# A gated-state attention block with a maxout FFN: start-up order, two subtractions moved to GpSimd, and the last outputs stored by quarters

## The chip, the cores and the metric

The kernel runs on one core of one Trainium2 chip. The metric is the device time of one launch in microseconds (us), the median of three runs.

## The reference

First a recurrence over 768 tokens for each of 4 batches and 8 heads (head size 48), then a feed-forward block of three products, an elementwise maximum and a fourth product over the 3072 tokens.

```python
f = 1.0 / (1.0 + np.exp(-f_logit))                 # B=4, H=8, S=768, D=48
for t in range(S):
    state = f[:, :, t, :, None] * state + np.einsum('bhd,bhe->bhde', k[:, :, t], v[:, :, t])
    y[:, :, t] = np.einsum('bhd,bhde->bhe', q[:, :, t], state)
x = np.ascontiguousarray(y.transpose(0, 2, 1, 3)).reshape(B * S, H * D)    # 3072 x 384
h = np.maximum(np.maximum(x @ w1, x @ w2), x @ w3)                         # 384 x 768 each
return h @ w_out                                                           # 768 x 384
```

## The kernel before

**Units and groups.** The attention part works in 24 *units* (u) of 64 tokens of two batches, all heads. A unit passes through `sigmoids` (the gates), `scan`, `after` (the scaled keys kh), `before` (the scaled queries qh), `keys` (keys turned for the state), `pairs` (key-query products, masked on VectorE), `values` (those times v), `sums` (the unit's addition to the state), `carry` (the old state times the unit's decay, on GpSimd), and `y_by_tokens` with `x_of_tokens` in the first four units, `finish` in the others. Four units make a group of 512 tokens, whose feed-forward block is put out piecemeal between the steps of later units: `fill(ns)` takes steps of a generator until their estimated cost has been used up. The first group has its own generator, `ffn_first`; the other five use `inputs_by_pairs` (the three input products by a scheme with fewer multiplications on sums and differences of weights and tokens) and `outputs_by_pairs` (the output product, likewise).

**Order.** The order of all instructions on every engine is the program's own, written out under a manual schedule; each engine executes its instructions in that order and waits on semaphores where a tile is not ready. DMAs are issued from SP's queue, a few from ACT's.

**Weights.** The weights arrive as 64-bit floating-point numbers and are turned to 32 bits in 24 pieces of 128 columns (n = 0 to 17 for w1, w2, w3 in turn, 18 to 23 for w_out). `round_begin(n)` is ACT's part: for n of 3 and over three instructions (L240, L241 on the upper words, L244 on the lower), for n under 3 only L244. `round_end(n)` is VectorE's part (L251 and L252 for n under 3, L254 for the others) and a sum on GpSimd (L258). `round_to(count)` runs, for every n up to count, round_begin of piece n+1 and round_end of piece n, and then the differences: w2 - w1 of a column block (n = 1, 4, 7 and so on) at once on GpSimd, w3 - w1 (n = 2, 5, 8 and so on) one piece later on VectorE, both by `apart` (L699). `ffn_first` uses them: its first product needs the difference of piece 1, its second that of piece 2, its third and fourth those of pieces 4 and 5, its fifth and sixth those of 7 and 8. The list `ROUNDED` tells how far the pieces are brought in each of its steps, and `TURNED` in which steps a block of w1 is transposed (`turn`, L720, copied by ACT in L721).

**Banks.** `ps_a` holds one tile, used by `pairs` and, in the first units, by `sums`; in units 0 and 1 the state is copied out of it by ACT (L442), in later ones added on VectorE (L444). `ps_tr` and `ps_f` have two tiles each, given out in turn. The 1x1 product at the head of `y_by_tokens` (L473) takes one of `ps_f`.

**The start.** The order around units 1 to 3 is written out by hand (L964 to L1004): y and x of unit 1, rounding of pieces 0 to 2, scan, pairs and carry of unit 3, and then the steps of `ffn_first`, one at each `fill(STEP)`.

**The end.** `outputs_by_pairs` multiplies blocks of 192 columns for two tiles of 128 tokens at a time into three banks: a of `ps_f`, b and c of `ps_tr`. `into(bank, p, ...)` puts tile pair p's block there, three matrix products each. Bank results are added to `partial` sums on VectorE (`add`, L619), on GpSimd (L655) or copied by ACT (L670) into `o_four`, four tiles of 128 x 384. `o_of(n, c)` is the column half c of the tiles n and n+2 in it. In the last group (`last`) the four tiles are written by `store` (two DMAs of 64 rows each) as soon as all columns of a tile are done: tiles 1 and 3 after L670, tile 0 and tile 2 after one half each of the last add; the second halves of tiles 2 and 3 go by ACT's queue, all others by SP's.

Of the kernel before, what the change touches and what calls it, by code (L numbers as in the profile page):

```python
# [46 lines left out]
C = 64  # L47
# [8 lines left out]
def kernel(  # L56
# [12 lines left out]
    nc = tc.nc  # L69
    B, H, S, D = q.shape  # L70
    HP = H // 2
    NU = B // 2 * (S // C)
    UT = 2 * C
    DM = H * D
    NK = DM // 128
    DFF = moe_w1.shape[1]
    NJ = DFF // 128
    GRP = 4
# [11 lines left out]
    def fast():  # L90
        ctx = ExitStack()
        with ctx:
# [64 lines left out]
            one = (nc.sync, nc.sync)  # L157
# [203 lines left out]
            def keys(u):  # L361

                if u < min(BY_ROWS, NU - 2):
                    kh = ready[u]["kh"]
                    tr_s = ps_tr.tile([UT, HP, 128], FP32, name="tr")
                    for hp in range(HP):
                        nc.tensor.transpose(tr_s[:, hp, :], kh[:, hp].rearrange("p a t -> p (a t)"), ident)
                    ks = work.tile([UT, H, DP], FP32, name="ks")
                    nc.scalar.copy(ks.rearrange("s h d -> s (h d)"), tr_s.rearrange("s a d -> s (a d)"))
                    ready[u]["ks"] = ks  # L370
# [51 lines left out]
            def sums(u):  # L422

                d, v_ld = ready[u], v_tiles[u % NLD]
                y = d["y"]
                if u < NU - 2:


                    apart = u < GRP
                    if apart:  # L430
                        y = ps_a.tile([128, 2, 512], FP32, name="a")
                    Y = HP * C
                    for hp in range(HP):
                        for par, a in FOUR:
                            s = slice(a * C, (a + 1) * C)
                            nc.tensor.matmul(y[par * DP:(par + 1) * DP, a, Y + hp * D:Y + (hp + 1) * D],  # L436
                                             lhsT=d["ks"][s, 2 * hp + par, :], rhs=v_ld[s, 2 * hp + par, 0:D],
                                             start=apart and hp == 0, stop=(hp == HP - 1), skip_group_check=True)
                    ds = y[:, :, Y:Y + HP * D]
                    new = states[u % 2].rearrange("p (a h) d -> p a (h d)", a=2)  # L440
                    if u < 2:
                        nc.scalar.copy(new, ds)  # L442
                    else:
                        nc.vector.tensor_tensor(new, ds, d["state"].rearrange("p (a h) d -> p a (h d)", a=2), op=ALU.add)  # L444
# [106 lines left out]
            def store(u, o):  # L551
                c, bp = divmod(u, 2)
                for a in range(2):
                    t0 = (2 * bp + a) * S + c * C
                    last = u >= NU - 2 and a
                    (nc.scalar if last else nc.sync).dma_start(out=out[t0:t0 + C, :], in_=o[a * C:(a + 1) * C, :])

            def outputs(hm, xT, i):
                p = bank()
# [16 lines left out]
            HJ, HD = NJ // 2, DM // 2  # L576
# [22 lines left out]
            def outputs_by_pairs(g, hm, xT):  # L599
                tile_of = lambda p, n: slice((2 * p + n) * UT, (2 * p + n + 1) * UT)  # L600
                A = lambda k, n: lambda p: hm[:, k::2, tile_of(p, n)]
                X = lambda n: lambda p: xT[:, 0:NK, tile_of(p, n)]
                s1, s2, s4 = (lambda p, t=t: t[:, :, p * UT:(p + 1) * UT] for t in s_mix)
                lin = [w_lin[:, :, n * HD:(n + 1) * HD] for n in range(2)]
                o_of = lambda n, c: o_four.rearrange("t (p n) c -> t n p c", p=2)[:, n, :, c * HD:(c + 1) * HD]
                last = g == NU // GRP - 1
                begun = set()

                def into(b, p, lhs, rhs):
                    for k in range(HJ):  # L610
                        nc.tensor.matmul(b[:, p * HD:(p + 1) * HD], lhsT=lhs(p)[:, k], rhs=rhs[:, k],  # L611
                                         start=id(b) not in begun, stop=(k == HJ - 1), skip_group_check=True)
                        begun.add(id(b))

                def read(b, n):
                    nc.scalar.copy(partial[n], b[:, 0:DM])  # L616

                def add(out, b, n, at=slice(0, 2)):
                    nc.vector.tensor_tensor(out[:, at], pairs_of(b[:, 0:DM])[:, at], pairs_of(partial[n])[:, at], op=ALU.add)  # L619

                COST = HJ * HD * COLUMN
                a, b, c = bank(), bank(True), bank(True)
                into(b, 0, X(0), lin[0])
                yield COST
                into(b, 1, X(0), lin[0])
                yield COST
                into(a, 0, A(0, 0), corner(0, 0))
                yield COST
                into(b, 0, A(1, 0), corner(1, 0))
                yield COST  # L630
                into(a, 1, A(0, 0), corner(0, 0))
                read(a, 0)
                yield COST
                into(b, 1, A(1, 0), corner(1, 0))
                add(o_of(0, 0), b, 0)
                yield COST
                into(a, 0, s2, w_mix[1])
                yield COST
                into(a, 1, s2, w_mix[1])
                read(a, 1)  # L640
                yield COST
                into(c, 0, s1, w_mix[0])
                yield COST
                into(c, 1, s1, w_mix[0])
                nc.scalar.copy(tops[:, 2], c[:, 0:DM])
                yield COST
                into(a, 0, A(0, 1), w_mix[2])
                yield COST
                into(a, 1, A(0, 1), w_mix[2])
                yield COST  # L650
                into(a, 0, X(1), lin[1])
                yield COST
                into(a, 1, X(1), lin[1])
                read(a, 2)
                nc.gpsimd.tensor_tensor(o_of(1, 1), pairs_of(tops[:, 2]), pairs_of(partial[2]), op=ALU.add)  # L655
                yield COST
                into(c, 0, X(0), lin[1])
                yield COST
                into(c, 1, X(0), lin[1])
                yield COST  # L660
                into(a, 0, A(1, 1), w_mix[3])
                yield COST
                into(a, 1, A(1, 1), w_mix[3])
                if g + 1 in packed:
                    sums_of_x(g + 1)
                yield COST
                into(a, 0, X(1), w_mix[4])
                yield COST
                into(a, 1, X(1), w_mix[4])
                nc.scalar.copy(o_of(1, 0), pairs_of(a[:, 0:DM]))  # L670
                if last:
                    for p in range(2):
                        store(g * GRP + 2 * p + 1, o_four[:, 2 * p + 1])
                yield COST
                into(c, 0, s4, corner(1, 1))
                if last:
                    add(o_of(0, 1), c, 1, slice(0, 1))
                    store(g * GRP, o_four[:, 0])
                yield COST
                into(c, 1, s4, corner(1, 1))  # L680
                if last:
                    add(o_of(0, 1), c, 1, slice(1, 2))
                    store(g * GRP + 2, o_four[:, 2])
                else:
                    add(o_of(0, 1), c, 1)
                    late.extend((g * GRP + i, o_four[:, i]) for i in (1, 3, 0, 2))
                yield COST

            late = []

# [4 lines left out]
            def apart(n, engine):  # L695
# [2 lines left out]
                piece = w_in[i][:, :, j * 128:(j + 1) * 128]  # L698
                engine.tensor_tensor(piece, piece, w_in[0][:, :, j * 128:(j + 1) * 128], op=ALU.subtract)  # L699

            rounded = [0]

            def round_to(count):

                for n in range(rounded[0], min(count, len(pieces))):
                    if n + 1 < len(pieces):
                        round_begin(n + 1)
                    round_end(n)
                    if n < 3 * NJ and n % 3 == 1:
                        apart(n, nc.gpsimd)  # L710
                    if n <= 3 * NJ and n and n % 3 == 0:
                        apart(n - 1, nc.vector)
                    rounded[0] = n + 1

# [212 lines left out]
            with tc.manual_schedule():  # L927
# [39 lines left out]
                values(1)  # L967
                y_by_tokens(1)
                keys(2)
                round_to(2)  # L970
                sums(1)
                x_of_tokens(1, xT)
                scan(3)
                pairs(2)
                after(3)
                carry(3)
                round_to(3)
                before(3)
                values(2)
# [2 lines left out]
                keys(3)  # L982
                sums(2)
                fill(STEP)
                y_by_tokens(2)
                pairs(3)
                fill(STEP)
# [342 lines left out]
```

## Time and profile before

| what | us |
|---|---|
| median of 3 runs (426.74 to 427.01) | 426.76 |
| the profiled execution, its own time | 427.35 |
| its span, first to last instruction | 425.5 |
| PE busy in the span (95%) | 405.3 |
| PE weight loads busy (80%) | 340.3 |
| VectorE (DVE) busy (62%) | 265.4 |
| GpSimd (POOL) busy (55%) | 232.8 |
| ScalarE (ACT) busy (42%) | 179.9 |

Busy shares are means over the whole span. The first 100 us, where the weights are turned and the first group waits for them, differ from the rest: ACT, VectorE and GpSimd are far busier there, and the chain of work that ended last passes through all of them, while from 100 us on it runs almost wholly through PE. The profiled execution took 1.85 us more than its span, which is what lies around the first and last instruction.

### The profile page before, as it was taken

The page shows a single profiled execution, that of the slowest core. Times are in us where ns is not written, and L with a number is a line of the kernel's source. Part 1 is how long each engine was busy: PE and PEld are TensorE (multiplying, and loading weights), DVE is VectorE, ACT ScalarE, POOL GpSimd, SP SyncE. Part 2 cuts the span into 40 slices and gives each one's busy share as a digit, 9 for nine tenths or more (in the row PEclk, how much of TensorE's full clock was granted, in tenths as well). Part 3 has the DMA queues.
Part 4 walks back from the last instruction along what each step waited for, and adds up shares of the span by engine and source line. Part 5 has one row for each costly group of instructions (what it writes and reads, how often), then busy time and mean ns, then how long its engine had stood idle before and what let it go on. Part 6 is the DMA issues. An engine that isn't in the chain of part 4 may idle for free.

```text
span 425.5 us, 11548 instructions
## 1 busy us (share of the span) xinstructions
PE 405.3 (95%) x4650; PEld 340.3 (80%) x4650; DVE 265.4 (62%) x517; ACT 179.9 (42%) x413; POOL 232.8 (55%) x260
## 2 busy tenths in 40 slices
PE   5988799899999999999999999999999999999993
PEld 4766665466567888998889988889988899988993
DVE  6986574952687699868789867888774720012300
ACT  2459566732114442425531444442264424576210
POOL 2178354541888676386586357566546960425600
PEclk9989999999999999999999999999999999999998
DMA  8988987771547753276645276634473011542003
GB/s 170 227 262 259 262 241 119 123 173 51 93 95 119 90 128 54 64 96 103 109 122 109 41 116 81 142 82 87 70 151 86 0 53 42 141 129 66 2 1 78
DMA packets 174617, 47.20 MB, mean 111 GB/s; under 512 B 154016, under 2 KB 172256, under 8 KB 174560
## 3 DMA queue, kind: packets, MB, share of 16 engines
q1 hardware_dynamic: 171216, 45.61, 51.6%
q10 hardware_dynamic: 3344, 0.81, 0.9%
q8 instruction: 37, 0.61, 0.6%
q14 instruction: 20, 0.16, 0.1%
HBM read 37.75 MB, written 4.72 MB: 100 GB/s over the span
## 4 chain that ended last, share of the span: by engine, by line
PE 86%; DVE 3%; SPq 3%; ACT 2%; DMA 2%; issue 1%; POOL 1%; DVEq 0%; POOLq 0%
PE p L819 19%; PE tr L819 16%; PE p L611 14%; PE tr L611 12%; PE p L564 6%; PE p L537 5%; PE p L728 3%; PE y L500 3%; PE y L411 3%; PE a L392 2%; DMA raw<-in_moe_w_dram 2%; SPq L174 2%; PE y L436 2%; PE tr L291 1%; SPq L164 1%
## 5 line engine op out<-in xcount | busy, mean ns | idle before, releaser
L819 PE MATMUL tr<-xT,placed 128*128 128x256 f32 x300 | 73.3, 385 | 0.0
L382 DVE STREAM_TRANSPOSE ks<-kh 32x128 f32<-32x128 f32 x224 | 67.7, 302 | 4.6 <-POOL kh L340 1.0
L819 PEld LDWEIGHTS tr<-xT,placed 128*128 128x128 f32 x300 | 55.6, 190 | 9.1 <-ACT hm L827 1.4
L819 PE MATMUL p<-xT,placed 128*128 128x256 f32 x180 | 45.0, 381 | 0.0
L819 PEld LDWEIGHTS p<-xT,placed 128*128 128x128 f32 x180 | 33.8, 190 | 4.7
L537 PE MATMUL p<-xT,w_in 128*128 128x256 f32 (+1 forms) x108 | 34.3, 458 | 2.9 <-DVE hm L750 2.2
L619 DVE TENSOR_TENSOR o<-tr,w_in 128x384 f32<-128x384 f32 (+1 forms) x11 | 5.7, 514 | 49.6 <-PE tr L611 44.3
L329 DVE TENSOR_TENSOR_SCAN r<-gate,from_one 128x520 f32<-128x520 f32 x24 | 31.3, 1306 | 8.3 <-ACT gate L308 5.3
L340 POOL TENSOR_TENSOR kh<-kt,r 128x512 f32<-128x512 f32 x16 | 28.8, 1798 | 10.6 <-DVE kt L296 10.6
L837 POOL TENSOR_TENSOR hm<-hm,rest_bits 128x512 f32<-128x512 f32 x15 | 22.7, 1512 | 19.1 <-ACT hm L827 19.1
L597 POOL TENSOR_TENSOR w_in<-hm 128x256 f32<-128x256 f32 x15 | 10.9, 727 | 40.5 <-DVE hm L870 40.5
L347 DVE TENSOR_TENSOR_SCAN prod<-gate,from_inv 128x520 f32<-128x520 f32 x24 | 32.5, 1355 | 0.0
L506 ACT COPY xT<-y 64x256 f32<-64x256 f32 (+1 forms) x60 | 22.1, 369 | 24.1 <-PE y L500 23.4
L395 DVE TENSOR_TENSOR at<-a,mask 128x512 f32<-128x512 f32 x24 | 16.5, 688 | 24.2 <-PE a L392 23.9
L258 POOL TENSOR_TENSOR w_in<-top_bits,rest_bits 128x384 uint32<-128x384 uint32 x18 | 21.8, 1211 | 15.5 <-DVE top_bits L254 8.8
L819 PE MATMUL p<-w_in,placed 128*128 128x256 f32 x120 | 30.0, 379 | 0.0
L862 DVE TENSOR_TENSOR hm<-tr,hm 128x512 f32<-128x512 f32 x15 | 10.2, 681 | 29.3 <-PE tr L819 19.3
L537 PEld LDWEIGHTS p<-xT,w_in 128*128 128x128 f32 x108 | 19.3, 190 | 10.7 <-issue 6.2
L655 POOL TENSOR_TENSOR o<-top_bits,w_in 128x384 f32<-128x384 f32 x5 | 5.1, 1015 | 41.6 <-ACT w_in L616 41.6
L616 ACT COPY w_in<-p 128x384 f32<-128x384 f32 x15 | 7.2, 479 | 47.1 <-PE p L611 47.1
L280 ACT ACTIVATE raw<-top_bits 128x384 f32<-128x384 f32 x48 | 25.2, 526 | 0.4
L819 PEld LDWEIGHTS p<-w_in,placed 128*128 128x128 f32 x120 | 22.8, 190 | 3.1
(153 smaller groups left out, 890.5 us busy)
## 6 DMA issues: line engine op xcount, KB each, us to landing
raw<-in_moe_w_dram SPq DMA_DIRECT2D x24, 384.0 KB, 4.2
v_ld<-in_v_dram SPq DMA_DIRECT2D x48, 96.0 KB, 3.2
placed<-in_moe_w_dram SPq DMA_DIRECT2D x12, 384.0 KB, 6.6
out_dram<-o SPq DMA_DIRECT2D x46, 96.0 KB, 2.4
placed<-in_moe_w_out_dram SPq DMA_DIRECT2D x6, 384.0 KB, 6.0
raw<-in_moe_w_out_dram SPq DMA_DIRECT2D x6, 384.0 KB, 3.4
f_ld<-in_f_logit_dram SPq DMA_DIRECT2D x32, 64.0 KB, 2.6
k_ld<-in_k_dram SPq DMA_DIRECT2D x32, 64.0 KB, 2.5
```

What stands on the lines that cost most here:

```text
L258: nc.gpsimd.tensor_tensor(dst, by(top), by(rest), op=ALU.add)
L280: nc.scalar.activation(over, size, AF.Relu, scale=(-1 / HI_MIN, 1.0)[step - 1], bias=(1.0, -HI_END * (1 - 2.0 ** -24))[step - 1], accum_ou ...
L329: nc.vector.tensor_tensor_scan(r[:, 0:LEN][:, ::-1], flat(gate)[:, ::-1], flat(from_one)[:, ::-1], 1.0, op0=ALU.mult, op1=ALU.max)
L340: (nc.vector if u < BY_ROWS else nc.gpsimd).tensor_tensor(kh.rearrange("p h a t -> p a h t"), kt, by_batch(r[:, 1:LEN + 1].rearrange("p (x ...
L347: nc.vector.tensor_tensor_scan(flat(prod), flat(gate_tiles[u % 2]), flat(from_inv[u % 2]), 1.0, op0=ALU.mult, op1=ALU.max)
L382: nc.vector.transpose(ks[n * 32:(n + 1) * 32, :, par, e0:e0 + 32], kh[p0:p0 + 32, :, a, t0:t0 + 32])
L506: nc.scalar.copy(xT[o, :, t0 + a * C:t0 + (a + 1) * C], y[i, a, 0:HP * C].rearrange("p (h t) -> p h t", h=HP))
L537: nc.tensor.matmul(p if w < TOK else p.rearrange("p (two t) -> p two t", two=2), lhsT=w_in[i][:, kt, j * 128:(j + 1) * 128], rhs=x[:, t.st ...
L564: nc.tensor.matmul(p[:, 0:DM], lhsT=lhsT, rhs=rhs, start=(n == 0), stop=(n == NJ + NK - 1))
L611: nc.tensor.matmul(b[:, p * HD:(p + 1) * HD], lhsT=lhs(p)[:, k], rhs=rhs[:, k], start=id(b) not in begun, stop=(k == HJ - 1), skip_group_c ...
L819: nc.tensor.matmul(b[:, j * HALF:(j + 1) * HALF], lhsT=w[:, (2 * n + j) * 128:(2 * n + j + 1) * 128], rhs=x, start=begin and j == 0, stop= ...
L837: nc.gpsimd.tensor_tensor(out(n, 0), out(n, 0), first, op=ALU.add)
```

## The change

Six edits. (1) In the start-up order, `sums(1)` comes first, then the rounding of piece 0, then `x_of_tokens(1)`, then that of piece 1; before, both roundings stood ahead of the two. So ACT's copies of the state and of x stand ahead of its part for piece 2, and the state's also ahead of that for piece 1. (2) `carry(3)` is put after two steps of `ffn_first` instead of ahead of piece 2. (3) The differences of pieces 2 and 8 are made on GpSimd directly after their sums, not one piece later on VectorE. (4) In the last group the last sum's second half goes through bank b (d = b), whose first use is the sum that `add(o_of(0, 0), b, 0)` reads; the first partial result of the same sum is copied by two half copies instead of one. (5) In the last group each column half of a tile pair is stored when it is done (`store_part`, two DMAs of 128 row pieces of 768 bytes): (0, 0), (1, 1), (1, 0), (0, 1), the last two pairs on SP's and ACT's queues together. (6) `store` itself uses SP's queue alone; `o_of` is moved out of the function.

```diff
@@ -552,8 +552,7 @@
                 c, bp = divmod(u, 2)
                 for a in range(2):
                     t0 = (2 * bp + a) * S + c * C
-                    last = u >= NU - 2 and a
-                    (nc.scalar if last else nc.sync).dma_start(out=out[t0:t0 + C, :], in_=o[a * C:(a + 1) * C, :])
+                    nc.sync.dma_start(out=out[t0:t0 + C, :], in_=o[a * C:(a + 1) * C, :])
 
             def outputs(hm, xT, i):
                 p = bank()
@@ -602,7 +601,6 @@
                 X = lambda n: lambda p: xT[:, 0:NK, tile_of(p, n)]
                 s1, s2, s4 = (lambda p, t=t: t[:, :, p * UT:(p + 1) * UT] for t in s_mix)
                 lin = [w_lin[:, :, n * HD:(n + 1) * HD] for n in range(2)]
-                o_of = lambda n, c: o_four.rearrange("t (p n) c -> t n p c", p=2)[:, n, :, c * HD:(c + 1) * HD]
                 last = g == NU // GRP - 1
                 begun = set()
 
@@ -633,16 +631,25 @@
                 yield COST
                 into(b, 1, A(1, 0), corner(1, 0))
                 add(o_of(0, 0), b, 0)
+                if last:
+                    store_part(g, 0, 0)
                 yield COST
                 into(a, 0, s2, w_mix[1])
                 yield COST
                 into(a, 1, s2, w_mix[1])
                 read(a, 1)
                 yield COST
+                d = b if last else c
                 into(c, 0, s1, w_mix[0])
                 yield COST
-                into(c, 1, s1, w_mix[0])
-                nc.scalar.copy(tops[:, 2], c[:, 0:DM])
+                if last:
+                    begun.discard(id(d))
+                    nc.scalar.copy(tops[:, 2, 0:HD], c[:, 0:HD])
+                into(d, 1, s1, w_mix[0])
+                if last:
+                    nc.scalar.copy(tops[:, 2, HD:DM], d[:, HD:DM])
+                else:
+                    nc.scalar.copy(tops[:, 2], c[:, 0:DM])
                 yield COST
                 into(a, 0, A(0, 1), w_mix[2])
                 yield COST
@@ -653,10 +660,12 @@
                 into(a, 1, X(1), lin[1])
                 read(a, 2)
                 nc.gpsimd.tensor_tensor(o_of(1, 1), pairs_of(tops[:, 2]), pairs_of(partial[2]), op=ALU.add)
+                if last:
+                    store_part(g, 1, 1)
                 yield COST
                 into(c, 0, X(0), lin[1])
                 yield COST
-                into(c, 1, X(0), lin[1])
+                into(d, 1, X(0), lin[1])
                 yield COST
                 into(a, 0, A(1, 1), w_mix[3])
                 yield COST
@@ -669,23 +678,30 @@
                 into(a, 1, X(1), w_mix[4])
                 nc.scalar.copy(o_of(1, 0), pairs_of(a[:, 0:DM]))
                 if last:
-                    for p in range(2):
-                        store(g * GRP + 2 * p + 1, o_four[:, 2 * p + 1])
+                    store_part(g, 1, 0, both)
                 yield COST
                 into(c, 0, s4, corner(1, 1))
                 if last:
                     add(o_of(0, 1), c, 1, slice(0, 1))
-                    store(g * GRP, o_four[:, 0])
-                yield COST
-                into(c, 1, s4, corner(1, 1))
+                yield COST
+                into(d, 1, s4, corner(1, 1))
                 if last:
-                    add(o_of(0, 1), c, 1, slice(1, 2))
-                    store(g * GRP + 2, o_four[:, 2])
+                    add(o_of(0, 1), d, 1, slice(1, 2))
+                    store_part(g, 0, 1, both)
                 else:
                     add(o_of(0, 1), c, 1)
                     late.extend((g * GRP + i, o_four[:, i]) for i in (1, 3, 0, 2))
                 yield COST
 
+            o_of = lambda n, c: o_four.rearrange("t (p n) c -> t n p c", p=2)[:, n, :, c * HD:(c + 1) * HD]
+
+            def store_part(g, n, c, queues=one):
+
+                for a in range(2):
+                    t0 = (2 * n + a) * S + 2 * g * C
+                    queues[a].dma_start(out=out[t0:t0 + 2 * C, c * HD:(c + 1) * HD].rearrange("(p r) c -> r p c", p=2),
+                                        in_=o_of(n, c)[a * C:(a + 1) * C])
+
             late = []
 
             def store_late():
@@ -698,6 +714,7 @@
                 piece = w_in[i][:, :, j * 128:(j + 1) * 128]
                 engine.tensor_tensor(piece, piece, w_in[0][:, :, j * 128:(j + 1) * 128], op=ALU.subtract)
 
+            AT_ONCE = (2, 8)
             rounded = [0]
 
             def round_to(count):
@@ -706,9 +723,9 @@
                     if n + 1 < len(pieces):
                         round_begin(n + 1)
                     round_end(n)
-                    if n < 3 * NJ and n % 3 == 1:
+                    if n < 3 * NJ and n % 3 == 1 or n in AT_ONCE:
                         apart(n, nc.gpsimd)
-                    if n <= 3 * NJ and n and n % 3 == 0:
+                    if n <= 3 * NJ and n and n % 3 == 0 and n - 1 not in AT_ONCE:
                         apart(n - 1, nc.vector)
                     rounded[0] = n + 1
 
@@ -967,13 +984,13 @@
                 values(1)
                 y_by_tokens(1)
                 keys(2)
+                sums(1)
+                round_to(1)
+                x_of_tokens(1, xT)
                 round_to(2)
-                sums(1)
-                x_of_tokens(1, xT)
                 scan(3)
                 pairs(2)
                 after(3)
-                carry(3)
                 round_to(3)
                 before(3)
                 values(2)
@@ -982,6 +999,7 @@
                 keys(3)
                 sums(2)
                 fill(STEP)
+                carry(3)
                 y_by_tokens(2)
                 pairs(3)
                 fill(STEP)
```

## The prediction

> **What bounds the kernel now.** I read the page's busy rows first: PE is busy 405.3 of 425.5 us, so an edit can only pay where PE waits. The list of waits of PE over the whole run (waiter <- releaser: us, times, longest) gives nearly all of them:
>
> ```profile
> PE p L537 <- DVE hm L750: 2.2, 3, 0.9
> PE a L392 <- ACT st L442: 1.8, 1, 1.8
> PE tr L489 <- ACT o L481: 1.3, 2, 0.7
> PE p L473 <- DVE st L444: 1.0, 1, 1.0
> PE p L537 <- POOL w_in L699: 0.6, 1, 0.6
> PE tr L611 <- DVE o L619: 0.5, 1, 0.5
> ```
>
> A wait of 5.0 us for the first input DMA stands ahead of these and isn't touched. All shown but the last lie before 84 us. From 84.4 to 417.7 us PE has no hole over 0.15 us, so what is won ahead of it is carried to the end, if nothing else binds. Next the timeline from 21 to 28 us (start, duration, engine):
>
> ```profile
> 22.50 0.56 ACT L244 ACTIVATE rest_bits<-raw 128x384 uint32<-128x384 uint32 x1 [0.38 <-DMA raw<-in_moe_w_dram]
> 22.97 0.45 ACT L442 COPY st<-a 128x384 f32<-128x384 f32 x1
> 23.47 0.75 PE L392 MATMUL a<-qh,kh 48*64 48x64 f32 x32 [1.80 <-ACT st L442]
> ...
> 25.07 1.01 POOL L699 TENSOR_TENSOR w_in<-w_in,w_in 128x384 f32<-128x384 f32 x1
> ...
> 26.43 1.15 POOL L357 TENSOR_TENSOR state<-st,ends 128x384 f32<-128x384 f32 x1
> ...
> 26.80 1.87 DVE L347 TENSOR_TENSOR_SCAN prod<-gate,from_inv 128x520 f32<-128x520 f32 x1
> ...
> 27.53 1.93 POOL L258 TENSOR_TENSOR w_in<-top_bits,rest_bits 128x384 uint32<-128x384 uint32 x1
> ```
>
> The state copy (L442), whose input was ready at 21.2, stands behind the half-words of piece 2 (L244), which wait for a DMA; pairs(2) needs that copy's bank. The windows, cut where the granted clock changes (PE, PEld, DVE, ACT, POOL busy; PEclk; DMA):
>
> ```profile
> 20.60:24.00 3.40, 1.60 (x67) 1.31 (x67) 2.88 (x4) 2.79 (x7) 1.81 (x2) 1.00 0.46 106
> 24.00:27.40 3.40, 3.40 (x45) 2.95 (x39) 3.02 (x7) 1.54 (x3) 3.24 (x4) 0.50 0.99 300
> 41.06:44.50 3.44, 2.03 (x40) 1.42 (x38) 1.80 (x2) 1.77 (x5) 1.24 (x2) 1.00 1.08 375
> ```
>
> After a stretch in which PE worked 1.60 of 3.40 us it ran at half clock for 3.4 us; after 2.03 of 3.44 it did not. Then DVE around 42 us:
>
> ```profile
> 41.38 1.34 DVE L699 TENSOR_TENSOR w_in<-w_in,w_in 128x384 f32<-128x384 f32 x1 [0.90 <-POOL w_in L258]
> 42.64 0.55 DVE L444 TENSOR_TENSOR st<-a,state 128x384 f32<-128x384 f32 x1
> ```
>
> The difference of piece 8 waits for its sum on GpSimd, and the new state queues behind it; PE, ready at 42.29, starts y of unit 3 (L473) at 43.33. Last, the end:
>
> ```profile
> 416.74 0.48 ACT L670 COPY o<-p 128x384 f32<-128x384 f32 x1 [5.37 <-PE p L611]
> 417.29 4.66 SPq L556 DMA_DIRECT2D out_dram<-o  x6
> 417.29 3.08 ACTq L556 DMA_DIRECT2D out_dram<-o  x2
> 417.79 0.36 DVE L619 TENSOR_TENSOR o<-tr,w_in 128x192 f32<-128x192 f32 x1 [14.08 <-PE tr L611]
> 418.20 1.24 PE L611 MATMUL tr<-w_out,w_in 128*128 128x192 f32 x6 [0.52 <-DVE o L619]
> 419.48 0.36 DVE L619 TENSOR_TENSOR o<-tr,w_in 128x192 f32<-128x192 f32 x1 [1.33 <-PE tr L611]
> ```
>
> The last add ends at 419.84, but SP is still issuing: six stores one after another, the last from 420.43 to 421.95. The last store packet ends at 423.20, and the program closes 2.3 us later.
>
> **What the skill says.** "TensorE: Matmul & The Clock Gate", section "What's actually happening": the clock depends on PE activity in free-running windows of about 3.4 us, half rate after an idle one. The trace agrees on the length (24.0 to 27.4), but half-idle sufficed. "SBUF — State Buffer", section "Who interferes with whom": a VectorE instruction with two SBUF inputs and a GpSimd one that reads SBUF shut each other out for a whole instruction. The trace agrees: the scan took 1.87 instead of 1.23 us beside L357, and the L258 behind it 1.93 instead of 1.00. "DMA: Bandwidth & Descriptors", section "Issuing engines are not separate DMA queues": a second issuing engine saves only issue time. Here that is 0.6 us per store. "PSUM — Partial Sum Buffer", section "PSUM bank collisions raise a hardware error": one engine must stay out of a bank that another reads. Hence the 0.52 us for which PE waits at 417.68.
>
> **Part 1, the start of the kernel.**
> *Order on ACT.* Nothing is added. L442 follows L369 (ends 21.55) and ends at 22.03; pairs(2) starts at 22.07, not 23.47. L244 of piece 1 slips by 0.4 us to 22.5, before the VectorE half it is added to (23.05): hidden. The copy of x (L490) ends at 22.9, not 23.8; its bank is wanted at 23.3 by q(3). The transposes of k(3) and q(3) end at 23.8. PE is then busy 2.8 of the 3.4 us to 24.0 and about 2.35 of the next, both over the 2.03 that kept the clock: no half rate. VectorE is not moved up (its scan waits behind piece 1's landing), so the masked pairs still end at 25.00; values(2) takes 25.05 to 26.2 (1.17 us as before at full clock). The first product needs piece 1's difference, ready at 26.08: it runs 26.2 to 27.7, before 27.73 to 29.3. **1.55 us** ahead here.
> *carry(3).* One L357 leaves its place ahead of piece 2's sum and comes after piece 6's: minus 1.15 us there, plus 0.83 to 1.15 later. Its readers come at 39 us and after: hidden.
> *Piece 2's difference.* L699 on VectorE 0.55 us goes; on GpSimd it costs 1.0 to 1.2 (rows of L699). GpSimd: L339 to 26.4, L258 of piece 2 shut out by the scan until 27.7, end 28.5; the difference to 29.7. The second product starts at 29.75, before 30.45: the lead shrinks to **0.7 us**, PE waiting some 0.8.
> *GpSimd to piece 7.* Pieces 3 and 4 and the difference of 4 end at about 33.1 (1.19, 1.0, 1.2 and gaps), so the third product starts 1.0 earlier than 34.15. Pieces 5, 6, carry(3), 7 and the difference of 7 end near 38.8, before 39.45. GpSimd has hardly any rest in this stretch, where before it waited 2.3 us.
> *ACT and the landings.* ACT's weight steps move up about 1.1 us until piece 9, which lands at 37.8 (piece 10 at 39.1) in the trace; SP's issues for these were held by the queue, not by compute, so they stay. Two groups of 1.48 us give the copy of turn(1) (L721) an end at 41.15, before 42.16. That copy frees y(3)'s bank.
> *Piece 8's difference.* VectorE loses the wait 0.90 and 1.34 us; state 3 is ready at 40.05. GpSimd gains 1.1 us, ending near 40.5; its reader, the sixth product, comes at 44.2: hidden. Late next is L721, so L473 starts at 41.2, not 43.33: **2.1 us** won. From here each wait (copy of o, xT, gate, scan, L750) follows PE or y(3). Piece 11 landed at 41.2 and was used at 46.2, piece 18 at 49.0 for 58.7, f of unit 5 at 49.8 for 58.2: loads have over 5 us to spare, and 2.1 us are carried on. Bounds: 0.3 (third product's lead lost to shut-outs) to 2.7.
>
> **Part 2, the end.** Two copies of 128x192 replace one L645 of 0.48 us (estimate 2 x 0.33, from 0.373 for 128x256) under 3 us of idle ACT: nothing. Into bank b the second half of the last sum waits only for an add that ended at 403.7: nothing. The hole of 0.52 us goes and the restart's slow 1.24 becomes 0.97: the last add ends at 419.06, **0.78 us** earlier. Of eight stores of 96 KB four now issue near 404 and 412.5, while PE works and SP, which waited from 401 to 417, has nothing else behind them. At 417.3 go one store on SP and one on ACT, at 419.1 the last two. A store issued on an idle queue landed 2.15 us after issue: about 421.35, last packet near 421.2, before 423.20. Rows are 768 bytes, not 1536; no such packet is in the trace. With 27 ns for 512 bytes and 112 for 1536 I take 60; were it 112, the last 256 packets on 16 engines need 0.9 us more. Part 2: **1.9 us**, bounds 0.8 to 2.4.
>
> **Sum.** 2.1 + 1.9 = 4.0 us off the profiled execution, 427.35 - 4.0 = 423.35 (span 421.5). That execution stands 0.59 over the median of 426.76; so the median becomes **422.8**.
>
> **Rivals.**
> *Start mostly eaten* (chance 0.20): shut-outs or a half-clock window leave 0.5 us. For: the 1.93 row, and GpSimd nearly full. Against: L721 gives y(3) some slack. 424.4.
> *End mostly eaten* (0.10): small packets, or the close bound by the instruction fetch that runs to 423.56 now; 0.8 remains. Against: that fetch follows SP's last issue, which moves up 2.2 us. 423.9.
> *GpSimd becomes the bound, slower* (0.06): ten large GpSimd instructions from 26.4 to the end of piece 7's difference take 1.15 us on average in my sum. From 1.64 (that end at 43.6) the start loses what the end wins; at 1.80, the longer row of L258 at 23 us, it ends at 45.2, the fifth product at 46.75, and y(3) is 3.4 late: 426.8 + 3.4 - 1.9 = 428.3. For: the shut-outs. Against: two of the thirteen large rows between 23 and 43 us exceed 1.4.
> *No effect* (0.03): the leads are lost to loads before 84 us and the close is fixed: 426.8. Against: loads above.
>
> **Numbers.** Likeliest 0.61, 422.8, own range 421.7 to 423.8. With the first two rivals the range is 421.6 to 424.8. About 0.2% (0.85 us) is what a measurement here can tell from no change: faster 0.91, same 0.03, slower 0.06.
>
> **What would show it.** In the new profile: the wait of L392 for L442 gone and PEclk full at 24 to 27; the first product near 26.2; L473 of unit 3 near 41.2 behind L721; no L699 on VectorE before 50 us except piece 5; L619's wait by PE gone; four L556 issues after 417 (shifted), last packet 2.1 us after the last add. Wrong if GpSimd's end of piece 7's difference is past 40 us, if the lead at 48.8 has dropped under 1 us by 100 us, or if the last store lands over 3 us after its issue.

## The result and the profile after

The median fell from 426.75 to 423.49 us (four runs each; 423.39 to 424.06 after). The ratio is 0.9925 with a 95% interval of 0.9908 to 0.9942, so the change saves 3.3 us, between 2.5 and 3.9. The profiled execution took 423.43 us over a span of 421.7 us; that of before took 427.35 over 425.5. Lines move by the edit: L699 is now L715, L750 L767, L721 L738, L611 L609, L619 L617, L670 L679, and the new stores are L702.

The waits of PE over the whole run, after (waiter <- releaser: us in total, times, longest):

```profile
PE p L537 <- DVE hm L767: 2.2, 3, 0.9
PE p L537 <- POOL w_in L715: 2.2, 2, 1.4
PE y L407 <- DVE at L395: 1.1, 1, 1.1
...
PE tr L489 <- ACT o L481: 0.6, 1, 0.6
```

The waits of L392 for the state copy, of L473 for the state and of L609 for the last add are gone. In their place stand two waits for differences on GpSimd, 1.4 us ahead of the second product and 0.7 ahead of the third, and one of 1.1 us of values(2) (L407) for the masked pairs. The windows after (PE, PEld, DVE, ACT, POOL busy; PEclk; DMA):

```profile
20.60:24.00 3.40, 2.79 (x75) 2.19 (x75) 2.65 (x6) 2.37 (x6) 2.23 (x2) 1.00 0.55 126
24.00:27.40 3.40, 2.77 (x41) 2.51 (x42) 3.37 (x6) 1.59 (x4) 2.63 (x4) 1.00 0.94 293
```

The clock is full there. The timeline around 40 us, after (start, duration, engine):

```profile
39.70 1.56 PE L537 MATMUL p<-xT,w_in 128*128 128x256 f32 x6
...
39.91 0.56 DVE L444 TENSOR_TENSOR st<-a,state 128x384 f32<-128x384 f32 x1
40.30 0.47 ACT L738 COPY w_in<-p 128x384 f32<-128x384 f32 x1
40.82 1.00 POOL L715 TENSOR_TENSOR w_in<-w_in,w_in 128x384 f32<-128x384 f32 x1
41.20 0.19 PE L473 MATMUL p<-st 128*1 128x1 f32 x2
```

The state is ready at 40.5, the copy of turn(1) at 40.8, and L473 follows the fifth product (39.70 and 1.56) without a hole: 41.20, where it was 43.33. The product that began at 48.80 begins at 46.67, and ACT's last copy begins at 414.63 instead of 416.74: the lead of 2.1 us is carried to the end. The end, from the timeline after:

```profile
401.62 15.94 SPq L702 DMA_DIRECT2D out_dram<-o  x6
...
414.63 0.48 ACT L679 COPY o<-p 128x384 f32<-128x384 f32 x1 [5.37 <-PE p L609]
415.14 2.47 ACTq L702 DMA_DIRECT2D out_dram<-o  x2
415.67 0.36 DVE L617 TENSOR_TENSOR o<-tr,w_in 128x192 f32<-128x192 f32 x1 [14.08 <-PE tr L609]
416.58 0.36 DVE L617 TENSOR_TENSOR o<-tr,w_in 128x192 f32<-128x192 f32 x1 [0.55 <-PE tr L609]
```

SP's six stores are spread over 16 us, the two adds lie 0.9 us apart instead of 1.7, and the last packet ends at 419.19, 2.25 us after the last add instead of 3.36.

### The profile page after: what moved, and what is told of

The parts are those of the page before. It is cut to its first block, busy times and chain, and to the rows that moved or that the text cites. A ratio compares the mean times of both kernels' runs of the same rounds, so it can differ in the third digit from the quotient of the medians.

```text
span 421.7 us, 11556 instructions
## 1 busy us (share of the span) xinstructions
PE 402.8 (96%) x4650; PEld 338.5 (80%) x4650; DVE 264.5 (63%) x515; ACT 180.2 (43%) x414; POOL 235.2 (56%) x262
## 4 chain that ended last, share of the span: by engine, by line
PE 86%; SPq 5%; DVE 3%; POOL 2%; issue 1%; ACT 1%; DMA 1%; DVEq 0%; POOLq 0%
PE p L836 19%; PE tr L836 16%; PE p L609 15%; PE tr L609 12%; PE p L563 6%; PE p L537 5%; PE p L745 3%; PE y L500 3%; PE y L411 3%; SPq L164 2%; PE a L392 2%; SPq L174 2%; PE y L436 2%; POOL w_in L258 1%; DMA placed<-in_moe_w_dram 1%
## 5 line engine op out<-in xcount | busy, mean ns | idle before, releaser
L617 DVE TENSOR_TENSOR o<-tr,w_in 128x384 f32<-128x384 f32 (+1 forms) x11 | 5.7, 515 | 48.8 <-PE tr L609 43.5
L596 POOL TENSOR_TENSOR w_in<-hm 128x256 f32<-128x256 f32 x15 | 10.9, 727 | 40.5 <-DVE hm L887 40.5
L506 ACT COPY xT<-y 64x256 f32<-64x256 f32 (+1 forms) x60 | 22.1, 369 | 24.1 <-PE y L500 23.4
L395 DVE TENSOR_TENSOR at<-a,mask 128x512 f32<-128x512 f32 x24 | 16.5, 688 | 24.2 <-PE a L392 23.9
L280 ACT ACTIVATE raw<-top_bits 128x384 f32<-128x384 f32 x48 | 25.3, 526 | 0.4
```

The source lines that it names most:

```text
L280: nc.scalar.activation(over, size, AF.Relu, scale=(-1 / HI_MIN, 1.0)[step - 1], bias=(1.0, -HI_END * (1 - 2.0 ** -24))[step - 1], accum_ou ...
L506: nc.scalar.copy(xT[o, :, t0 + a * C:t0 + (a + 1) * C], y[i, a, 0:HP * C].rearrange("p (h t) -> p h t", h=HP))
```

## The experiments

Ratios are to the kernel before on the same chip. Two numbers are read from each trace. *L473* is the start of the first matrix product of y of unit 3. *Tail* is the time from the start of ACT's last copy (L670, L679) to the end of the span. With the whole new end it is 7.05 to 7.08 us in six traces; with the old end it is 8.76 to 8.92 in three and 9.18 and 9.38 in e1 and e5, the two in which piece 8's difference is moved. Why these two are longer is not known, and so a difference against an old end is known to some 0.6 us only. The first input's DMA lets PE begin between 4.9 and 5.5 us, so the table also has L473 counted from there.

| kernel | ratio, interval | L473 | from first input | tail |
|---|---|---|---|---|
| before | 1 | 43.33 | 38.34 | 8.80 |
| after | 0.9925, 0.9908 to 0.9942 | 41.20 | 36.21 | 7.08 |
| e1 start alone | 0.9953, 0.9935 to 0.9972 | 42.27 | 36.96 | 9.18 |
| e2 end alone | 0.9958, 0.9943 to 0.9972 | 42.74 | 37.77 | 7.06 |
| e3 before again | 1.0009, 0.9998 to 1.0020 | 43.42 | 38.17 | 8.76 |
| e4 order alone | 0.9997, 0.9982 to 1.0012 | 42.98 | 38.05 | 8.92 |
| e5 piece 8 alone | 0.9956, 0.9943 to 0.9969 | 41.27 | 36.24 | 9.38 |
| e6 after, piece 8 back | 0.9950, 0.9931 to 0.9968 | 42.66 | 37.71 | 7.08 |
| e7 after, piece 2 back | 0.9899, 0.9882 to 0.9917 | 42.03 | 36.53 | 7.06 |
| e8 after, carry(3) back | 0.9928, 0.9911 to 0.9945 | 41.51 | 36.55 | 7.06 |
| e9 piece 8 and end | 0.9915, 0.9903 to 0.9928 | 41.48 | 36.31 | 7.05 |
| e10 one bank | 0.9927, 0.9915 to 0.9940 | 41.14 | 36.20 | 7.83 |
| e11 old stores | 0.9939, 0.9926 to 0.9952 | 41.07 | 35.82 | 8.56 |
| e12 last quarter by tiles | 0.9895, 0.9878 to 0.9912 | 40.81 | 35.81 | 6.23 |

### e1: the start alone

```diff
+ sums(1); round_to(1); x_of_tokens(1, xT); round_to(2)    # for round_to(2); sums(1); x_of_tokens(1, xT)
+ carry(3) two fills later;  AT_ONCE = (2, 8)
```

> The kernel before with the start-up edits alone: sums(1) and x_of_tokens(1) ahead, carry(3) later, differences of pieces 2 and 8 on GpSimd; the end as before. Theory: the start and the end add up, and the start is worth 2.1 us: the product that began at 48.8 us begins near 46.7, PEclk stays full from 24 to 27.4 us, and the median is 2.1 us lower (ratio 0.995). Rival (the half-clock stretch of the profiled execution is not in the timed ones): the profile still shows 2.1 us, but the median falls by 1.4 us only, since the median of the whole change fell by 3.3 us where the profiled executions differ by 3.9. Rival (end does most): under 0.8 us.

The ratio says 2.0 us (1.2 to 2.8), which does not tell 2.1 from 1.4. The clock was full from 24 to 27.4. The product of 48.8 us began at 47.75 only. The profiled execution was the slowest of the six (426.67 us, median 425.50), and its weights were late: piece 9 landed at 38.8, after the whole change at 37.1. Then another wait appeared, in the waits of PE from 38 to 45 us:

```profile
PE p L473 <- ACT w_in L722: 0.7, 1, 0.7
```

That is the copy of turn(1), behind the weight steps on ACT. Of the other traces only that of e7 has it.

### e2: the end alone

```diff
+ d = b if last else c;  store_part(...) four times;  start as before
```

> The kernel before with the edits of the end alone: last sum through two banks, last outputs by quarters. Theory: the last sum's second half follows without the hole of 0.52 us, the last add comes 0.8 us earlier, the last packet ends 2.2 us after it instead of 3.4; PE's position at 48.8 us is unchanged; median lower by 1.7 us (ratio 0.996), and with the start's gain this makes the whole. Rival (the two do not add): under 1.0 us or over 2.5 us.

As the theory said: 1.8 us by the ratio, adds 0.9 us apart, last packet 2.25 us after the last add, tail 7.06, shorter by 1.7 us or more than in any of the five traces with the old end. The product of 48.8 us came at 49.27; this execution had half clock from 45.0 to 48.4. Start and end together give 3.8 us by the two ratios, the whole change 3.3, within both intervals.

### e3: the kernel before, profiled again

```diff
  no edit
```

> The kernel before, unchanged, profiled a second time. Theory (half clock is a state of single executions): the stretch of half clock after the wait of L392 is absent or elsewhere, the span is some 0.6 us shorter than 425.5 and the product at 48.8 us begins about 0.6 earlier. Rival (it belongs to the kernel): half clock again near 24 us, span within 0.3 us of 425.5. Ratio 1.000 in either.

Half clock was absent, as theory had it, but nothing was saved by that: PE was busy 402.9 us instead of 405.3, yet the span is 425.6 and the product came at 48.90. Its windows and VectorE's timeline:

```profile
20.60:24.00 3.40, 1.71 (x62) 1.25 (x64) 2.82 (x4) 2.57 (x6) 1.95 (x2) 1.00 0.41 89
24.00:27.40 3.40, 3.40 (x69) 3.01 (x60) 3.24 (x7) 1.54 (x3) 3.24 (x5) 1.00 0.99 311
```

```profile
41.47 1.34 DVE L699 TENSOR_TENSOR w_in<-w_in,w_in 128x384 f32<-128x384 f32 x1 [0.89 <-POOL w_in L258]
42.73 0.54 DVE L444 TENSOR_TENSOR st<-a,state 128x384 f32<-128x384 f32 x1
```

PE was hardly busier up to 24 us (1.71 us against 1.60), yet the clock stayed full, and the first product began at 26.38 instead of 27.73. By 43 us all of this had run into the same wait: the state behind piece 8's difference. The wait was 1.4 us here and 1.0 in the other execution, where half clock had made PE late. So, counted from the first input, a lead of 1.6 us at the first product shrank to 0.2 at L473 while the wait stood.

### e4: the order on ACT alone

```diff
+ sums(1); round_to(1); x_of_tokens(1, xT); round_to(2)
```

> The kernel before with the ACT order alone: sums(1) and x_of_tokens(1) ahead of the roundings of pieces 0 and 1; carry(3) and the differences of pieces 2 and 8 as before. Theory: L392 starts near 22, values(2) a little after 25, the first product near 26.2, but the new state of unit 3 still queues behind piece 8's difference on VectorE, whose sum on GpSimd cannot come before piece 8 and 9 are through ACT; the lead at 48.8 us is about 1.0 us and the median 0.5 to 1.1 us lower. Rival (order is all of the start's gain): 2.1 us at 48.8 us. Rival (order is eaten wholly): under 0.3 us.

L392 began at 21.76 and the first product at 25.28, as forecast, but the ratio is 0.9997 and the lead at 48.8 us 0.35 us. Counted from the first input it is 0.29 us against the kernel before and 0.13 against e3, so the rival that it is eaten wholly holds. The waits of PE from 20 to 36 us, first of e3, then of e4, show where it went:

```profile
PE a L392 <- ACT st L442: 1.7, 1, 1.7
PE p L537 <- DVE w_in L699: 1.3, 1, 1.3
...
```

```profile
PE p L537 <- DVE w_in L699: 1.7, 1, 1.7
PE y L407 <- DVE at L395: 0.7, 1, 0.7
```

The wait for the state copy is exchanged for waits for the masked pairs and for piece 2's difference; both are VectorE's, which the order doesn't move up. At L473 the wait is 1.5 us:

```profile
PE p L473 <- DVE st L444: 1.5, 1, 1.5
```

### e5: piece 8's difference alone

```diff
+ AT_ONCE = (8,)                                 # kernel before otherwise
+ if n < 3 * NJ and n % 3 == 1 or n in AT_ONCE: apart(n, nc.gpsimd)
+ if n <= 3 * NJ and n and n % 3 == 0 and n - 1 not in AT_ONCE: apart(n - 1, nc.vector)
```

> The kernel before with one edit: the difference of piece 8 on GpSimd right after its sum. Theory (that wait is the gate, the rest of the start decides how far the lead reaches): L473 of unit 3 no longer waits for the state; it starts when the fifth product ends, near 42.2 us, and the lead at 48.8 us is 1.0 to 1.3 us, median 1.1 us lower (ratio 0.9975). Rival (this edit is all of the start's gain): lead 2.0 us, ratio 0.995. Rival (moving it back to GpSimd only shifts the wait): under 0.3 us.

My theory of 1.1 us fell; the rival holds: this one edit gives 1.9 us by the ratio (1.3 to 2.4), and L473 begins at 41.27 as after the whole change. From its timeline:

```profile
39.77 1.56 PE L537 MATMUL p<-xT,w_in 128*128 128x256 f32 x6
...
39.91 0.56 DVE L444 TENSOR_TENSOR st<-a,state 128x384 f32<-128x384 f32 x1
...
41.27 0.19 PE L473 MATMUL p<-st 128*1 128x1 f32 x2
```

The wait of L392 for the state copy is still in this kernel (1.1 us), and its fifth product begins at 39.77 all the same, 0.07 us from that of the changed kernel. Another way to the same end, to put the state ahead of the difference on VectorE, was not tried.

### e6: the changed kernel with piece 8 back on VectorE

```diff
- AT_ONCE = (2, 8)
+ AT_ONCE = (2,)
```

> The changed kernel with the difference of piece 8 alone put back on VectorE, one piece later. Theory (gate): L473 waits for the state again, near 43 us; of the start's 2.1 us at most 0.5 are left, and against the kernel before only the end's 1.8 us and those remain (ratio 0.995 to 0.996). Rival (order, carry and piece 2 carry the start): L473 near 41.5, ratio 0.992.

The gate is confirmed from the other side. The fifth product starts as early as ever (39.66), and the wait is back, 41.22 to 42.66, as its waits from 38 to 45 us say:

```profile
PE p L473 <- DVE st L444: 1.4, 1, 1.4
```

What is left, 2.1 us by the ratio (1.4 to 3.0), is what the end gives.

### e7: the changed kernel with piece 2 back on VectorE

```diff
- AT_ONCE = (2, 8)
+ AT_ONCE = (8,)
```

> The changed kernel with the difference of piece 2 alone put back on VectorE, behind piece 3. Theory (GpSimd is full between 26 and 40 us and the move of piece 2 costs it 1.25 us): the second product starts within 0.5 us of 29.8, the third 0.5 to 1.0 us earlier than 33.3, and L473 then waits for the copy of turn(1), so that at most 0.4 us are won: ratio to the kernel before 0.991 to 0.9925. Rival (piece 2 on GpSimd earns a part of the gain): the second product near 30.5, L473 0.5 later, ratio 0.994.

The ratio is lower than theory allowed, and the trace does not show why. Its execution was the slowest of the six (424.31 us, median 423.07): the first input came at 5.5 us and piece 9 landed at 38.5. L473 did wait for the copy of turn(1), as theory had it; the wait is seen at its weight load, in the waits from 38 to 44 us:

```profile
PEld p L473 <- ACT w_in L738: 0.5, 1, 0.5
```

Counted from the first input, the second product came at 24.7 us and the third at 28.4, after the whole change at 24.8 and 28.3; L473 came at 36.53 against 36.21. Theory's earlier third product is not there. The interval ends at 0.9917 and that of the changed kernel, from other runs, begins at 0.9908. e8, which ran on the same chip and differs from the changed kernel by carry(3) alone, has 0.9928, from 0.9911. Whether piece 2 on VectorE is better stays open; that moving it to GpSimd earned anything is not seen.

### e8: the changed kernel with carry(3) back

```diff
+ carry(3) after after(3), ahead of round_to(3)
```

> The changed kernel with carry(3) alone back ahead of piece 2's sum. Theory: its 1.15 us on GpSimd go ahead of piece 2's sum, so that the second product starts near 30.8 and the third near 34.4; the fifth product's wait for the difference of piece 7 doesn't come (carry is gone from in front of it), L473 starts 0.3 to 0.8 us later than 41.2: ratio to the kernel before 0.9935. Rival (its place is hidden): the same as the changed kernel, 0.9925, L473 within 0.2 us.

The second product waits longer, as forecast in kind (its waits of PE from 24 to 36 us):

```profile
PE p L537 <- POOL w_in L715: 2.8, 2, 2.1
...
```

It began at 30.00, not 30.8, and the ratio is that of the changed kernel. L473 is 0.3 us later, more than the rival's 0.2, but less than the 0.4 us by which the traces of after, e10, e11 and e12, which have the same start, differ among themselves (35.81 to 36.21 from the first input). As far as the ratio can tell, the place of carry(3) is hidden.

### e9: piece 8 and the end, without the rest

```diff
  start order, carry(3) and piece 2 as before
+ AT_ONCE = (8,);  end as in the changed kernel
```

> The kernel before with the difference of piece 8 on GpSimd and the edits of the end; the order on ACT, carry(3) and piece 2 as before. Theory, changed after the runs so far (all of the start's gain is the wait of 1.44 us of L473 for the state behind piece 8's difference; order, carry and piece 2 earn nothing): the same as the whole change, ratio 0.992 to 0.993, L473 near 41.3 to 42.0 without a wait over 0.7 us. Rival (the other edits help in most executions, only not in the one profiled): 0.9945 or more.

Ratio 0.9915 against 0.9925, intervals overlapping, and L473 is at 41.48 without a wait: piece 8's difference and the end make the whole gain, as far as these intervals tell.

### e10: the last sum in one bank

```diff
- d = b if last else c
+ d = c                                          # one copy of the first partial sum, as before
```

> The changed kernel with both halves of the last sum in bank c again; stores by quarters kept. Theory: the hole of 0.52 us before the last six matrix products returns and the last add comes 0.8 us later against the add before it (1.7 us between the two adds, not 0.9); the last packet still ends 2.2 to 2.3 us after the last add: 0.8 us worse than the changed kernel, ratio to the kernel before 0.994 to 0.995. Rival (the bank's part is hidden behind the stores): within 0.2 us of the changed kernel.

The timeline of its end:

```profile
415.59 0.36 DVE L617 TENSOR_TENSOR o<-tr,w_in 128x192 f32<-128x192 f32 x1 [14.08 <-PE tr L609]
416.01 1.24 PE L609 MATMUL tr<-w_out,w_in 128*128 128x192 f32 x6 [0.52 <-DVE o L617]
417.29 0.36 DVE L617 TENSOR_TENSOR o<-tr,w_in 128x192 f32<-128x192 f32 x1 [1.34 <-PE tr L609]
```

The hole is back, the adds are 1.7 us apart, the last packet ends 2.24 us after the last add, and the tail is 0.75 us longer than after. The ratio, 0.9927, is lower than the forecast 0.994 to 0.995, and so are those of e9 and e11, which ran together with it. Against e9, which has both banks and ran on the same chip, e10 is 0.0012 higher, 0.5 us, and the two intervals leave room for 0.75.

### e11: two banks, stores by whole tiles

```diff
- store_part(g, 0, 0); store_part(g, 1, 1); store_part(g, 1, 0, both); store_part(g, 0, 1, both)
+ store(tile 1); store(tile 3); ... store(tile 0); ... store(tile 2)      # six DMAs on SP, two on ACT, as before
```

> The changed kernel with two banks kept and the last outputs stored by whole tiles, six on SP and two on ACT, as before. Theory (SP's six issues of 0.6 us set the end, from L670's copy on, so that an earlier last add finds the queue full): the adds are 0.9 us apart, but the last packet ends some 4 us after the last add, and the end is within 0.3 us of the kernel before: of the end's 1.8 us nearly all is gone, ratio 0.995 to 0.9965. Rival (each edit has its own share, 0.8 and 1.1 us): 0.994.

The timeline:

```profile
415.03 4.53 SPq L556 DMA_DIRECT2D out_dram<-o  x6
...
416.43 0.36 DVE L618 TENSOR_TENSOR o<-tr,w_in 128x192 f32<-128x192 f32 x1 [0.55 <-PE tr L610]
```

The adds come as early as after the change, but SP is at its six stores until 419.6: they follow one another without rest, one of them took 1.3 us instead of 0.6, and the last is issued at 419.0, 2.2 us after the last add has ended. From the rows of `out_dram` (durations in ns, min/median/max; first and last start in us):

```profile
L556 SPq DMA_DIRECT2D out_dram<-o x6: 473/601/1313, 415.0 to 419.0; - x6
```

The last packet ends 4.0 us after the last add. That the last store waits for SP's queue, as theory said, is thus shown. What it costs is less clear. The tail is 8.56 us, 0.24 less than in the one trace of before, 0.6 less than in e1, which has the same start, and 0.2 to 0.8 less than in all five traces with the old end. So the second bank alone is worth something between 0.2 and 0.8 us, and the rival's 0.8 is not excluded. The ratio, 0.9939, is the rival's number; against e9 on the same chip the stores by tiles cost 0.0024, 1.0 us, where the tails differ by 1.5.

### e12: the last quarter tile by tile

```diff
  add(o_of(0, 1), c, 1, slice(0, 1))
+ store_tile(g, 0, 0, 1)     # 48 KB on SP and 48 KB on ACT: tile 0's half
  into(d, 1, s4, corner(1, 1)); add(o_of(0, 1), d, 1, slice(1, 2))
- store_part(g, 0, 1, both)
+ store_tile(g, 1, 0, 1)     # tile 2's half
```

> The changed kernel with the last quarter stored tile by tile: two DMAs of 48 KB after the first half of the last add, two after the second. Theory (the last pair's data movement adds to the fixed landing): only half the bytes are left after the last add, so its last packet ends 1.7 to 1.9 us after it instead of 2.25, 0.3 to 0.5 us better than the changed kernel. Rival (the landing is a fixed time): within 0.1 us. Rival (two more issues per queue delay the last): 0.2 to 0.6 us worse.

```profile
415.64 1.40 SPq L710 DMA_DIRECT2D out_dram<-o  x2
415.64 1.42 ACTq L710 DMA_DIRECT2D out_dram<-o  x2
416.16 0.36 DVE L617 TENSOR_TENSOR o<-tr,w_in 128x192 f32<-128x192 f32 x1 [0.55 <-PE tr L609]
```

The last packet ends 1.81 us after the last add, 0.44 earlier than after the change, as forecast, and the tail is 0.85 us shorter; the other 0.4 us lie between the last packet and the end (2.1 us here, 2.5 after), and what made those longer was not tried. With a median of 422.39 us and a ratio of 0.9895 this is the lowest of the kernels run, though the interval overlaps those of e7 and of the changed kernel. The tail was read from one execution, the fastest of the six; all six traces with the whole new end have 7.05 to 7.08, so 6.23 lies well outside what they vary.

## Why the prediction was right, and where not

**The total.** A median of 422.8 us was forecast, and 423.49 was measured, inside the stated 421.7 to 423.8. 4.0 us were forecast off the profiled execution, and between the two profiled executions 3.92 went. Between the medians only 3.26 did. The term that was mis-sized is the start, 2.1 us. The wait that its edits remove measures 1.44 to 1.47 us in e2, e3, e4 and e6; and over all traces, counted from the first input, the five with this wait have L473 at 37.71 to 38.34 us, mean 38.01, and the nine without at 35.81 to 36.96, mean 36.29. So the start gives 1.4 to 1.7 us, which the ratios of e1 and e5 (2.0 and 1.9 us) include in their intervals, and with 1.72 for the end it is 3.2 to 3.4 in all. The agreement of 4.0 with 3.92 is in part luck: both were read against the same execution. That execution, from which 2.1 was worked out, has the latest L473 of the five. The step that carried its lateness into the median was "That execution stands 0.59 over the median of 426.76; so the median becomes **422.8**": the offset was taken off while part of it sat in the gain.

**Order on ACT: wrong.** "**1.55 us** ahead here" compared an execution at half clock with one at full clock. At full clock the first product begins at 25.5 to 26.4 us with the old order (e2, e3, e5, e9) and at 25.3 to 26.5 with the new one. In all fourteen traces it follows values(2) (L407) without a hole, and with the new order values(2) waits for the masked pairs, as in the changed kernel's timeline:

```profile
24.63 1.17 PE L407 MATMUL y<-v_ld,at 64*64 64x48 f32 x32 [1.10 <-DVE at L395]
24.65 1.01 POOL L715 TENSOR_TENSOR w_in<-w_in,w_in 128x384 f32<-128x384 f32 x1
25.73 1.56 PE L537 MATMUL p<-xT,w_in 128*128 128x256 f32 x6
```

The masked pairs stand behind a scan on VectorE, and piece 1's difference on GpSimd (L715) is ready only at 25.66; the order on ACT moves neither up. The pairs end at 24.2 to 25.1 us with the old order at full clock and at 24.1 to 25.4 with the new one. The prediction had both of these times (25.00, 26.08); what it missed is that the old order meets them too, once PE isn't at half clock. e4 shows no gain from the order alone.

Nor did the half clock belong to the hole of L392: e3 has the hole and full clock, and e4 has no such hole and half clock at 30.0. The Trainium skill calls the windows free-running ("TensorE: Matmul & The Clock Gate", section "What's actually happening"), and this case agrees: half clock was found from 24.0, 30.0 and 45.0 us, each in one execution only and each time 3.4 us long. The page names an idle window as the cause; here PE was busy 1.60, 1.71 and 1.66 of the 3.4 us before. Yet e3 passed through 3.4 us with 1.36 us busy (from 41.5), and no half clock followed. That the place of the window's edge decides would explain this; no run here tests it.

**carry(3) and piece 2: hidden, and more so than thought.** The second product's start (29.75 forecast, 29.79 measured), the third's (33.15, 33.31) and L473's (41.2, 41.20) came as worked out, and still these edits earn nothing that is seen: e5 and e9 reach the same without them. GpSimd did fill up: its ten large instructions took 1.22 us on average (1.15 forecast), and piece 7's difference ended at 39.46 instead of 38.8, still ahead of the fifth product, so the slower rival did not come.

**Piece 8: right place, wrong share.** The wait of L473 for the state was taken at its 1.04 us in the one trace, with the rest of the 2.1 put down to the earlier steps. It is 1.44 us when PE isn't late, and nothing else of the start is seen in e5, e6 and e9 beyond what landings vary. "Late next is L721" holds only where piece 9 lands late (e1, e7). After the change the copy was ready at 40.8 and L473 followed the fifth product itself, so it is luck that 41.2 was met so closely.

**The end: right, 1.9 forecast and 1.72 measured.** The last add came 0.79 us earlier (0.78 forecast); a 768-byte packet took 59 ns in the median (60); the last packet ended 2.25 us after the add (2.1), and the close took 2.5 instead of 2.3 us. The reserve for slower packets was 16 times 52 ns, 0.83 us and not 0.9; it was not needed. Split, the stores by quarters give 0.9 us or more with one bank (e10 against the old ends), the second bank 0.75 more (after against e10), and 0.2 to 0.8 without these stores (e11). The sum has no term for a last store that waits for its queue, as in e11; whether the two edits thereby need each other is not decided by these traces.

## What to carry to other kernels

When several waits lie in a row on the engine that bounds a kernel, begin with the last one that every path runs into: a lead ahead of it counts only as far as that wait's releaser moves too. Profile the starting kernel twice before sizing a gain from one trace: here the second profile had no half clock and the same span, which showed that the 1.55 us forecast for the order were not there to win. At the end of a program, count the issues on each DMA queue after the last computed tile, and keep the bytes behind the last instruction few.

## What was not expected of the hardware

A stretch of half clock 3.4 us long moved between executions or was absent, and the one at 24.0 us, which delayed the first product by over 1 us, left L473 within 0.2 us of where it is without it (38.34 against 38.17 us from the first input). Halving the bytes of the last stores, from 96 to 48 KB on each of two queues, shortened the time from last add to last packet by 0.44 us.
